# Attention's loads in another order on SyncE's queue: one weight block later, six weight blocks ahead of keys and values

## The chip, the cores and the metric

The kernel runs on one core of one Trainium2 chip. The metric is the device time of one execution in microseconds (us). Three executions of the kernel before took 513.55, 513.63 and 513.99 us; their median is 513.63 us.

## The reference, cut to what matters

Three stages follow one another: a decayed linear attention over 2 batches x 8 heads, a gated product through dense weights, and a mixture of 8 experts with top-1 routing.

```
# attention, in blocks of 64 positions
intra = (qb @ kb^T * Dmask) @ vb          inter = (qb * lam_pow) @ kv_state
out   = intra + inter                     kv_state = lam^64 * kv_state + (kb * rev_pow)^T @ vb
# dense stage, x is (1536, 512)
h = ((x @ w1) * (x @ w2)) @ w3            x2 = h @ w_out
# experts: argmax of x2 @ w_gate, capacity 384 rows each
out = gate_w * relu(xe @ e1) @ e2
```

## The kernel before, in words

**Attention** takes its 16 (batch, head) pairs two heads at a time, so eight iterations `it` = 0 to 7, each over all 768 positions. An iteration needs two loads of 768 KB, called by `load_qkv` (L304): `tqk` (queries and keys, transposed, L306) and `tkv` (keys and values, L308). Both have three buffers, so `tqk` and `tkv` of iteration `it + 2` are issued in iteration `it`, after the last use of the buffer by iteration `it - 1`. "Pair 4" below is the fourth pair of loads, that of iteration 3; it is issued in iteration 1.

An iteration has two halves. `part1(it)` multiplies queries by keys (L391), masks the scores (L400 on VectorE), and builds the states from the decayed keys `kd` (L413, L421). `part2(it - 1)` multiplies scores by values (L439), adds the state's part (L453), and splits the result into a rounded part `xth` (ScalarE, L462) and a rest `xtl` (VectorE, L463). The decayed keys `kd` of the next iteration are made on ScalarE from `tkv` (L362).

**Weights are prepared beside it.** The dense weights come as 64-bit numbers, in blocks of 512 KB (L122). The chunks stand in a list: blocks 0 to 7 are `woi` (w_out), blocks 8 to 23 `w3i`, then `w`. `Feed.load(n)` (L152) issues the next n blocks, on SyncE's queue like `tqk` and `tkv`. It keeps the list's order and stops where a block would need a staging buffer whose block has not been converted yet in program order: there are four such buffers, and blocks 0 to 3 have buffers of their own. `Feed.tick` (L166) moves every block in flight one step on and starts the next one. The steps of a block: two ScalarE instructions read it (L132, L133), one tick later two on VectorE (L135, L138) finish it and so free the buffer, one tick later ScalarE and GpSimd split it (L142, L143). For w_out blocks TensorE then transposes (L219), ScalarE copies (L222), and TensorE multiplies by the gate's weights (L227). `TICKS` (L37) places the ticks: none in iteration 0, one at the end of iteration 1, and from iteration 2 on one in the middle of `part1` and one at the end. So block 0 starts in iteration 1, blocks 1 and 2 in iteration 2, blocks 3 and 4 in iteration 3, and so on to blocks 11 and 12. `LOADS` (L36) says how many blocks are issued behind the pair loads of each iteration; block 0 is issued before the loop.

All engines work through their instructions in program order. SyncE's instructions are nothing but these loads, in the order in which the program calls them; an instruction that waits holds up all behind it. Every SyncE load also waits until the load eight places ahead of it, or nearly so, has landed.

**After attention** (from 59.56 us on) come the product w3 x w_out (L295 to L297), the gated stage, routing and the experts, all dense matmuls.

Of the kernel before, what the change touches and what calls it, by code (L numbers as in the profile page):

```python
# [32 lines left out]
NW = (2, 1, 1, 1, 1, 1, 1, 1)  # L33
HOOK = 6
OVER = 7
LOADS = (1, 2, 2, 2, 2, 2, 2, 0)  # L36
TICKS = ((0, 0, 0, 0), (0, 0, 0, 1)) + ((1, 0, 0, 1),) * 6 + ((0, 0, 1, 0),)  # L37
XBW = 265

# [2 lines left out]
def tile_moe_chain(ctx, tc, cap, qk, kv, w12, w3i, woi, wgi, e1i, e2i, c32, c16, zero, out):  # L42
# [21 lines left out]
    def bank():  # L64
        return ps.tile([P, 512], F32, tag="b", name="bank")
# [138 lines left out]
    feed = Feed()  # L204

    def run_bg(n=1):
        for _ in range(n):
            feed.tick()
# [29 lines left out]
    def u_ready(it):  # L238
        u = bank()
        for jb in range(4):  # L240
            nc.tensor.matmul(
                u[:, jb * NE : (jb + 1) * NE],
                it.up[:, jb * P : (jb + 1) * P],
                gsum,
                start=True,
                stop=True,
            )
        it.us = us = u[:, 0 : 4 * NE].rearrange("p (j e) -> p j e", e=NE)
        uh, ul = it.view(it.hi)[:, :, 512:520], it.view(it.lo)[:, :, 512:520]
        nc.vector.tensor_copy(uh, us)  # L250
        nc.vector.tensor_tensor(ul, us, uh.bitcast(F32), op=ALU.subtract)
# [13 lines left out]
    for w, e, j in turn[0:2] + turn[4:5] + turn[2:4] + turn[5:]:  # L265
        tag = min(until, key=until.get)
        it = Item((e1i, e2i)[w][e, j], "p3g" if tag == "x" else "ring", tag)
# [32 lines left out]
    with pool("att", 2, side="right") as ap, pool("att1", side="right") as a1:  # L300
        slots["att"] = ap
        loads = {}

        def load_qkv(it):  # L304
            tqk = ap.tile([P, 2, S], F32, tag="qk", name="tqk", bufs=3)
            nc.sync.dma_start(tqk, qk[it])  # L306
            tkv = ap.tile([P, 2, NC, P], F32, tag="kv", name="tkv", bufs=3)
            nc.sync.dma_start(tkv, kv[it])  # L308
            loads[it] = (tqk, tkv)
# [3 lines left out]
        dmask = a1.tile([P, 4, P], F32, name="dmask")  # L313
        nc.sync.dma_start(c32_sb, c32)
        load_qkv(0)
        load_qkv(1)
        feed.load(1)
        warm = tmp.tile([P, 512], F32, tag="t", name="warm").bitcast(F16)[:, 0:512]
# [38 lines left out]
        def decay_keys(it):  # L357
            if it == 8:
                return
            kds[it] = ap.tile([P, NC - 1, P], F32, tag="kd", name="kd", bufs=1)  # L360
            for h in range(2):
                nc.scalar.activation(  # L362
                    kds[it][:, :, h * 64 : h * 64 + 64],
                    loads[it][1][:, 0, 0 : NC - 1, h * 64 : h * 64 + 64],
                    AF.Copy,
                    scale=dmask[:, (it // 2 * 2 + h) % 4, P - 1 : P],
                )
# [63 lines left out]
        def part2(it, ticks, qs, at, st):  # L431
            pair, b = divmod(it, 2)
            tkv = loads[it][1]
            os = [bank(), bank()]
            for cc in range(NC):
                half, c = divmod(cc, 3)
                for h in range(2):
                    hs = slice(h * 64, h * 64 + 64)
                    nc.tensor.matmul(  # L439
                        os[half][hs, c * P : (c + 1) * P],  # L440
                        tkv[:, 1, cc, hs],
                        at[:, h, cc, :],
                        start=c == 0,
                        stop=cc == 0,
                        skip_group_check=True,
                    )
            for half, o in enumerate(os):
                for c in range(3):
                    cc = half * 3 + c
                    for h in range(2):  # L450
                        hs = slice(h * 64, h * 64 + 64)
                        if cc:
                            nc.tensor.matmul(  # L453
                                o[hs, c * P : (c + 1) * P],
                                st[hs, cc - 1, :],
                                qs[hs, cc, :],
                                start=False,
                                stop=True,
                                skip_group_check=True,
                            )  # L460
                xh, xl = xt[2 * b + half]
                nc.scalar.copy(xh[:, pair, :], o[:, 0:G])  # L462
                nc.vector.tensor_tensor(  # L463
                    xl[:, pair, :], o[:, 0:G], xh[:, pair, :].bitcast(F32), op=ALU.subtract
                )
                if half == 0:
                    run_bg(ticks[2])

        prev = None
        for it in range(8):  # L470
            cur = part1(it, TICKS[it])
            if prev is not None:
                part2(it - 1, TICKS[it], *prev)
            if it + 2 < 8:
                load_qkv(it + 2)
            prev = cur
            feed.load(LOADS[it])
            if it == 2:
                nc.scalar.dma_start(wg_sb, wgi)
            if TICKS[it][3]:  # L480
                feed.tick(mid=lambda: decay_keys(it + 1))
            elif it + 1 < 8:
                decay_keys(it + 1)
            if wo_it[0].done == 4 and not hasattr(wo_it[0], "us"):
                u_ready(wo_it[0])
# [401 lines left out]
    for e in range(NE):  # L887
# [12 lines left out]
        for s in range(nmain):  # L900
            acc = bank()
            ss = slice(s * P, (s + 1) * P)
            for fb in range(8):
                it = e2_it[2 * e + fb // 4]
# [90 lines left out]
```

## Time and profile before

| | us |
|---|---|
| median of three executions | 513.63 |
| the profiled execution | 513.23 |
| its span in the trace | 511.1 |
| TensorE busy in the span | 497.0 |
| ScalarE busy / VectorE busy | 242.7 / 265.0 |
| first matmul after attention (L295) | 59.56 |

The page gives busy time by engine, the span in forty slices, the queues, and the costliest groups of instructions. TensorE is busy for 97% of the span. Almost all the time it is not lies in the first 60 us, the attention, and in the last 10. What is asked here happens in the first 60 us, so the trace is read there by stretches and in order of time.

### The profile page before, as it was taken

How to read it: one execution, taken by the hardware profiler on the slowest of the kernel's cores; microseconds unless marked ns; L12 is line 12 of the kernel's file. 1: busy time of each engine (PE TensorE's matmuls, PEld its weight loads, DVE VectorE, ACT ScalarE, POOL GpSimd, SP SyncE). 2: the span in 40 equal slices, each digit the busy share in tenths (PEclk: the TensorE clock that was granted, in tenths of full speed). 3: DMA queues.
4: the chain of work that ended last, by engine and by line, in shares of the span. 5: the costliest groups of instructions: out<-in, count | busy, mean ns of one | idle time of the engine just before them, and what ended most of it. 6: DMA issues, size and time to landing. Idle time of an engine off the chain costs nothing. (4 is left out here: it accounts for less than half of the span.)

```text
span 511.1 us, 9558 instructions
## 1 busy us (share of the span) xinstructions
PE 497.0 (97%) x3805; PEld 468.5 (92%) x3805; DVE 265.0 (52%) x576; ACT 242.7 (47%) x485; POOL 126.5 (25%) x124
## 2 busy tenths in 40 slices
PE   7999999999999999999999999999999999999993
PEld 4888999999999999999999999989989898989892
DVE  4998885668333223322332463768474746647410
ACT  2697987789211221122112423656455555646310
POOL 4356564446200000000020004404313040410101
PEclk9999999999999999999999999999999999999998
DMA  8999466557911000100010215587665667564200
GB/s 323 415 410 379 150 223 215 182 193 239 332 39 43 1 0 23 43 1 0 13 53 0 83 65 163 191 272 251 217 214 206 232 203 259 167 241 165 81 1 34
DMA packets 24529, 80.80 MB, mean 158 GB/s; under 512 B 3642, under 2 KB 5692, under 8 KB 24480
## 3 DMA queue, kind: packets, MB, share of 16 engines
q1 hardware_dynamic: 18976, 70.35, 38.9%
q0 software_dynamic: 3344, 7.85, 4.7%
q10 hardware_dynamic: 2160, 1.94, 1.1%
q8 instruction: 32, 0.52, 0.5%
q14 instruction: 17, 0.14, 0.1%
HBM read 74.84 MB, written 10.54 MB: 167 GB/s over the span
## 5 line engine op out<-in xcount | busy, mean ns | idle before, releaser
L97 DVE TENSOR_TENSOR wlo<-st,whi 128x512 fp32r<-128x512 f32 x128 | 82.1, 685 | 16.8 <-ACT whi L95 16.7
L295 PE MATMUL bank<-xtl,whi 128*128 128x384 f32 x256 | 87.1, 340 | 0.0
L297 PE MATMUL bank<-xth,wlo 128*128 128x384 f32 x256 | 86.4, 337 | 0.0
L296 PE MATMUL bank<-xth,whi 128*128 128x384 f32 x256 | 85.8, 335 | 0.0
L95 ACT CAST whi<-st 128x512 fp32r<-128x512 f32 x128 | 73.0, 621 | 15.8 <-PE bank L297 10.9
L787 PE MATMUL bank<-xdl,whi 128*128 128x256 f32 x256 | 72.4, 283 | 1.1 <-PEq L834 0.8
L787 PE MATMUL bank<-xdh,whi 128*128 128x256 f32 x256 | 72.2, 282 | 0.0
L787 PE MATMUL bank<-xdh,wlo 128*128 128x256 f32 x256 | 72.1, 282 | 0.0
L143 POOL TENSOR_TENSOR wlo<-t,whi 128x512 fp32r<-128x512 f32 x40 | 51.9, 1297 | 52.1 <-ACT whi L142 46.5
L295 PE MATMUL bank<-wxl,gh 128*128 128x264 f32 (+1 forms) x192 | 55.9, 291 | 0.0
L296 PE MATMUL bank<-wxh,gh 128*128 128x264 f32 (+1 forms) x192 | 54.2, 282 | 0.0
L297 PE MATMUL bank<-wxh,gl 128*128 128x264 f32 (+1 forms) x192 | 54.1, 282 | 0.0
L564 DVE TENSOR_TENSOR a_sb<-bank,a_sb 128x384 f32<-128x384 f32 x32 | 17.8, 557 | 66.9 <-PE bank L297 66.3
L295 PE MATMUL bank<-wlo,hh 128*128 128x512 f32 x128 | 51.1, 399 | 0.0
L297 PE MATMUL bank<-whi,hl 128*128 128x512 f32 x128 | 50.3, 393 | 0.0
L787 PEld LDWEIGHTS bank<-xdl,whi 128*128 128x128 f32 x256 | 48.5, 189 | 1.9 <-PEq L834 1.2
L296 PE MATMUL bank<-whi,hh 128*128 128x512 f32 x128 | 50.0, 390 | 0.0
L800 DVE SCALAR_TENSOR_TENSOR hl<-bank,hh 128x512 fp32r<-128x512 f32 x32 | 22.1, 690 | 53.3 <-ACT hh L799 53.3
L718 POOL DMA_INDIRECT out_dram<-y,idx x16 | 16.1, 1006 | 134.3 <-ACT y L920 104.8
L787 PEld LDWEIGHTS bank<-xdh,whi 128*128 128x128 f32 x256 | 48.3, 189 | 0.3
L787 PEld LDWEIGHTS bank<-xdh,wlo 128*128 128x128 f32 x256 | 48.4, 189 | 0.0
L295 PEld LDWEIGHTS bank<-xtl,whi 128*128 128x128 f32 x256 | 48.1, 188 | 0.0
(109 smaller groups left out, 1003.2 us busy)
## 6 DMA issues: line engine op xcount, KB each, us to landing
st<-e1i SPq DMA_DIRECT2D x32, 512.0 KB, 5.2
st<-e2i SPq DMA_DIRECT2D x32, 512.0 KB, 4.0
st<-w3i SPq DMA_DIRECT2D x16, 512.0 KB, 4.7
st<-w SPq DMA_DIRECT2D x16, 512.0 KB, 4.1
tqk<-qk SPq DMA_DIRECT2D x8, 768.0 KB, 11.1
tkv<-kv SPq DMA_DIRECT2D x8, 768.0 KB, 9.3
st<-woi SPq DMA_DIRECT2D x8, 512.0 KB, 10.1
out_dram<-zero SPq DMA_DIRECT2D x1, 3072.0 KB, 14.3
```

What stands on the lines that cost most here:

```text
L95: nc.scalar.copy(h, s)
L97: nc.vector.tensor_tensor(lo, s, h.bitcast(F32), op=ALU.subtract)
L143: nc.gpsimd.tensor_tensor(lo, t, h.bitcast(F32), op=ALU.subtract)
L295: nc.tensor.matmul(acc, wh, rl, start=first, stop=False)
L296: nc.tensor.matmul(acc, wh, rh, start=False, stop=False)
L297: nc.tensor.matmul(acc, wl, rh, start=False, stop=last)
L564: nc.vector.tensor_tensor(a_sb, acc, a_sb, op=ALU.mult)
L718: nc.gpsimd.indirect_dma_start(out=out, out_offset=bass.IndirectOffsetOnAxis(ap=idx[:, col : col + 1], axis=0), in_=src, in_offset=None, b ...
L787: nc.tensor.matmul(o, w[:, k, :], x[:, k, :], start=m == 0 and k == 2 and x is xl, stop=m == 1 and k == 1 and w is lo, skip_group_check=True,)
L800: nc.vector.scalar_tensor_tensor(hl, acc, 0.0, hh.bitcast(F32), op0=ALU.max, op1=ALU.subtract)
```

## The change

`LOADS` gives iteration 1 one block instead of two and iteration 7 one instead of none. `load_qkv` gets an argument: that many blocks are issued between `tqk` and `tkv`. In iterations 3, 4 and 5 all blocks of the iteration (two) go there, so ahead of `tkv`; elsewhere they stay behind the pair.

```
-LOADS = (1, 2, 2, 2, 2, 2, 2, 0)
+LOADS = (1, 1, 2, 2, 2, 2, 2, 1)
...
-        def load_qkv(it):
+        def load_qkv(it, first=0):
             tqk = ap.tile([P, 2, S], F32, tag="qk", name="tqk", bufs=3)
             nc.sync.dma_start(tqk, qk[it])
+            feed.load(first)
             tkv = ap.tile([P, 2, NC, P], F32, tag="kv", name="tkv", bufs=3)
             nc.sync.dma_start(tkv, kv[it])
...
+            ahead = LOADS[it] if 2 < it < 6 else 0
             if it + 2 < 8:
-                load_qkv(it + 2)
+                load_qkv(it + 2, ahead)
             prev = cur
-            feed.load(LOADS[it])
+            feed.load(LOADS[it] - ahead)
```

SyncE's queue from pair 4 to pair 5 before (`st0_261` holds blocks 2 and 3, `st_347` block 4, `st_349` block 5; `tqk_257` and `tkv_259` are pair 4, the other two pair 5):

```order
L306 DMA tqk_257<-qk 128x1536
L308 DMA tkv_259<-kv 128x1536
L122 DMA st0_261<-woi 128x1024 x2
L306 DMA tqk_343<-qk 128x1536
L308 DMA tkv_345<-kv 128x1536
L122 DMA st_347<-woi 128x1024
L122 DMA st_349<-woi 128x1024
```

The same stretch of SyncE's queue after (`tqk_342` and `tkv_344` are now pair 5):

```order
L306 DMA tqk_257<-qk 128x1536
L309 DMA tkv_259<-kv 128x1536
L122 DMA st0_261<-woi 128x1024
L306 DMA tqk_342<-qk 128x1536
L309 DMA tkv_344<-kv 128x1536
L122 DMA st0_261<-woi 128x1024
L122 DMA st_347<-woi 128x1024
```

Block 3 has moved from ahead of pair 5 to behind it, and block 5 to the next iteration.

SyncE's queue around the last two pairs before (`tqk_545` and `tkv_547` are pair 7, `tqk_655` and `tkv_657` pair 8; `st_549` is block 8, `st_659` block 9, `st_661` block 10):

```order
L306 DMA tqk_545<-qk 128x1536
L308 DMA tkv_547<-kv 128x1536
L122 DMA st_549<-w3i 128x1024
L306 DMA tqk_655<-qk 128x1536
L308 DMA tkv_657<-kv 128x1536
L122 DMA st_659<-w3i 128x1024
L122 DMA st_661<-w3i 128x1024
```

The same after (`st_545` is block 7, `st_547` block 8, `st_657` block 9, `st_659` block 10; the pairs are `tqk_543`, `tkv_549` and `tqk_655`, `tkv_661`):

```order
L306 DMA tqk_543<-qk 128x1536
L122 DMA st_545<-woi 128x1024
L122 DMA st_547<-w3i 128x1024
L309 DMA tkv_549<-kv 128x1536
L306 DMA tqk_655<-qk 128x1536
L122 DMA st_657<-w3i 128x1024
L122 DMA st_659<-w3i 128x1024
L309 DMA tkv_661<-kv 128x1536
```

Blocks 9 and 10 now stand ahead of pair 8's `tkv`, blocks 7 and 8 ahead of pair 7's. The instructions of the other engines keep their order.

## Rows read from the trace of the kernel before

**Rows 1.** Part 2 of the page: DMA busy tenths in 40 slices of the span.

```profile
DMA  8999466557911000100010215587665667564200
```

**Rows 2.** Windows: length; PE, PEld, DVE, ACT, POOL busy (instructions); PEclk; DMA share; GB/s.

```profile
28.61:35.46 6.85, 6.84 (x105) 5.71 (x105) 6.02 (x12) 6.32 (x13) 4.68 (x4) 1.00 1.02 409
35.46:43.09 7.63, 7.63 (x113) 6.69 (x112) 7.42 (x15) 7.41 (x15) 4.37 (x3) 1.00 1.03 412
...
60.00:160.00 100.00, 100.00 (x741) 99.81 (x740) 58.05 (x122) 62.66 (x126) 39.04 (x31) 1.00 0.57 192
```

**Rows 3.** Waits of TensorE, 60 to 512 us: us in total, times, longest.

```profile
PE bank L787 <- PEq L834: 0.8, 1, 0.8
```

**Rows 4.** Waits of ScalarE, 16 to 60 us.

```profile
ACT bank L132 <- DMA st<-w3i: 2.6, 1, 2.6
```

**Rows 5.** Timeline of SyncE's queue: start us, us, engine, line, operation, out<-in, count.

```profile
15.03 0.33 SPq L308 DMA_DIRECT2D tkv<-kv  x1
15.40 0.90 SPq L122 DMA_DIRECT2D st<-woi  x2
...
20.11 0.33 SPq L308 DMA_DIRECT2D tkv<-kv  x1
20.48 1.04 SPq L122 DMA_DIRECT2D st<-woi  x2
...
34.34 0.33 SPq L122 DMA_DIRECT2D st<-w3i  x1
...
40.04 0.33 SPq L308 DMA_DIRECT2D tkv<-kv  x1
40.47 37.37 SPq L122 DMA_DIRECT2D st<-w3i  x15
```

**Rows 6.** DMA issues near 15.03, 15.40, 20.11, 40.47 us: KB each, us to landing.

```profile
tkv<-kv SPq DMA_DIRECT2D x1, 768.0 KB, 8.0
...
st<-woi SPq DMA_DIRECT2D x1, 512.0 KB, 8.9
...
tkv<-kv SPq DMA_DIRECT2D x1, 768.0 KB, 9.5
...
st<-w3i SPq DMA_DIRECT2D x1, 512.0 KB, 8.5
```

**Rows 7.** Timeline, 25.6 to 28.7 us: columns of rows 5, [idle before <-releaser].

```profile
25.62 0.61 ACT L142 CAST whi<-t 128x512 fp32r<-128x512 f32 x1
26.13 0.64 ACT L132 ACTIVATE bank<-st 128x512 f32<-128x512 f32 x1
...
27.59 1.09 PE L219 MATMUL bank<-c_sb,t 128*128 128x128 f32 x8
27.86 1.00 DVE L463 TENSOR_TENSOR xtl<-bank,xth 128x384 fp32r<-128x384 f32 x2
...
28.61 1.61 PE L391 MATMUL bank<-tqk 64*128 64x128 f32 x24
```

**Rows 8.** Timeline, 33 to 54 us, the same columns.

```profile
33.10 1.41 PE L453 MATMUL bank<-qs,state 64*64 64x128 f32 x20
...
37.61 1.03 PE L413 MATMUL bank<-tkv,kd 128*64 128x64 f32 x19
...
47.45 1.41 PE L453 MATMUL bank<-qs,state 64*64 64x128 f32 x20
...
48.96 0.65 ACT L132 ACTIVATE bank<-st 128x512 f32<-128x512 f32 x1 [2.63 <-DMA st<-w3i]
...
51.21 1.60 PE L391 MATMUL bank<-tqk 64*128 64x128 f32 x22 [0.92 <-DVE xtl L463]
...
53.31 0.82 PE L413 MATMUL bank<-tkv,kd 128*64 128x64 f32 x19
```

**Rows 9.** Windows at the end of the span, columns of rows 2.

```profile
503.00:504.00 1.00, 0.03 (x1) 0.00 (x0) 0.38 (x1) 0.47 (x1) 0.00 (x0) 1.00 0.00 0
...
506.00:507.00 1.00, 0.00 (x0) 0.00 (x0) 0.00 (x0) 0.00 (x0) 0.00 (x0) 0.55 0.38 146
```

## The prediction, made before the changed kernel ran

> **What bounds the kernel now.** I read the forty slices first. The DMA engines are busy nine tenths and more through slices two to four, the first 50 us, and far less behind [rows 1]. Next the windows: through attention the DMA share is 1.02 at 409 GB/s, so the queue never runs dry there, and ScalarE is busy for 6.32 of 6.85 us and 7.41 of 7.63 us of two iterations [rows 2]. Then TensorE behind attention: from 60 us on it is busy 100.00 of 100.00 us [rows 2], and its longest wait down to the end is 0.8 us [rows 3]. So whatever the change does to the end of attention moves the end of the kernel by the same amount; behind it nothing can hide or give back a shift.
>
> Inside attention two limits stand close together: ScalarE's chain, and the order in which the full queue delivers. The waits of ScalarE show where the second one wins: it waits 2.6 us once for a w3 block [rows 4], the one whose reading starts at 48.96 us [rows 8]. That is block 9: blocks 8 and 9 start at the end of iteration 5 and in iteration 6.
>
> The queue delivers in the order of issue. The `tkv` of pair 4 is issued at 15.03 us and lands 8.0 us later, at 23.0; block 2 is issued at 15.40 and lands 8.9 us later, at 24.3 [rows 5, 6]. The distance of 1.3 us is the block's own transfer: 524,288 B at 409 GB/s is 1.28 us. A `tqk` or `tkv` of 786,432 B takes 1.92 us. While the queue is full, a landing time is therefore set by the bytes ahead of it, whatever order those bytes have among themselves.
>
> **The change part by part.** Nothing is added or removed on the computing engines. Only landing times move.
>
> *Block 3 goes behind pair 5.* Before, the queue holds block 2, block 3, `tqk` and `tkv` of pair 5; after, block 2, `tqk`, `tkv`, block 3. These are the same bytes, so block 3 now lands when that `tkv` landed: issued at 20.11, 9.5 us to landing, 29.6 us [rows 5, 6]. The issue is no limit: block 3 is issued right behind the `tkv`, near 20.5 us, with some nine microseconds of transfers ahead. Its reader is ScalarE's L132 in iteration 3, which started at 26.13 without a wait, just as the instruction ahead of it ended (25.62 plus 0.61 is 26.23) [rows 7]. So ScalarE now waits from 26.2 to 29.6, 3.4 us. Behind it in ScalarE's order stand L133 and the two `xth` casts; VectorE's `xtl`, at 27.86, needs the casts, and TensorE's next scores, at 28.61, need the banks that `xtl` frees [rows 7]. All three engines stand still; TensorE has only the transposes of 27.59 to do, which end at 28.68. The whole chain moves by 3.4 us. What can it win back before the next wait? At most the idle time of ScalarE, its busiest engine, in the next two iterations: 14.48 us less 13.73 busy [rows 2], 0.75 us. It is idle there because it waits for the others, which move as well, so I take nothing back. Ends: 2.65 us, and 3.5 us with the re-start of VectorE behind the casts. Value: 3.4 us.
>
> *Blocks 5 to 10 ahead of three `tkv` loads.* Block 9 landed at 40.47 plus 8.5, 48.97 us [rows 5, 6]. It now stands ahead of the last `tkv`, so 1.92 us fewer bytes precede it: 47.05 us. Its reader was ready 2.63 us before 48.96, at 46.33 [rows 8], and with the 3.4 us above comes at 49.7. The wait of 2.63 us is gone, wholly. What was it worth? Not 2.63: while ScalarE stood, TensorE went on with L453 at 47.45, on which the casts depend in any case. Compare the same piece of two iterations: from L453 to L413 it took 37.61 less 33.10, 4.51 us, without a wait, and 53.31 less 47.45, 5.86 us, with it [rows 8]. The difference, 1.35 us, is my value. Ends: the 0.92 us that TensorE itself shows before L391 [rows 8], and the whole 2.63.
>
> *The `tkv` loads that come later.* Those of pairs 6 and 7 have one block more ahead of them than before, 1.28 us; their readers come 3.4 us later. That of pair 8 has two more, 2.56 us: it landed just ahead of block 9, at 47.7, and now lands at 50.2, while TensorE used its product at 53.31 [rows 8] and will do so about two microseconds later. No cost. Without the shift of 3.4 us, each would be near its reader.
>
> *Waits on SyncE.* Block 8 needs the buffer of block 4 and now stands ahead of pair 7's `tkv` and pair 8's `tqk`; blocks 9 and 10 stand ahead of pair 8's `tkv`. Block 8 was issued at 34.34, when its buffer came free [rows 5], so now at 37.7. The queue then still holds what ends with block 7: behind block 3 (29.6) come block 4, `tqk`, two blocks, `tkv`, `tqk`, block 7, or 4 x 1.28 + 3 x 1.92 = 10.9 us, so it lands until 40.5. With 2.8 us of work left the queue doesn't run dry, and those behind the wait are not late. No cost; if the cover went, the readers named above would still have some two microseconds.
>
> *Iteration 7's block* is issued a little earlier or later in a queue that is no longer full. Nothing.
>
> **Sum.** 3.4 less 1.35 is 2.05 us more. The profiled execution took 513.23 us, its span 511.1, with 2.1 us around it; it would take 515.3. The median is 0.40 us above that execution, so the median becomes 513.63 + 2.05 = 515.7 us.
>
> **The rivals.** *All of the old wait comes back.* If the engines are so tightly tied that ScalarE's idle 2.63 us was lost entirely, and ScalarE's 0.75 us is won back, the cost is 2.65 less 2.63, nothing; with 3.4, it is 0.8. The middle is 0.4 us, so 514.0. For it: ScalarE is nearly full. Against it: the comparison of the two iterations, and the 0.92 us.
>
> *Block 3 isn't late.* Were the queue to serve it ahead of the 1.5 MB of pair 5, or were the queue not full at 20 us, the wait at 26.2 would not arise; what is left is the old wait's 1.35 us: 512.3, faster. It decides at one point: whether block 3 lands by 26.2. Against it stand the DMA share of 1.02 and the landings in order, 1.3 us apart [rows 2, 6]. If only part of the lateness went, the balance lies at a wait of 1.35 us, block 3 landing at 27.6.
>
> *TensorE's clock falls in the new gap.* TensorE ends its transposes at 28.7 and has nothing until about 32. At the end of the span the last matmul is over in the window from 503, the granted clock is still 1.00 there, and in the window from 506 it is 0.55 on the mean [rows 9], so within it the clock goes to 1.2 GHz. A gap of about 3.3 us is as long as that stretch. An iteration's piece of 3 us of matmuls at half the clock would take 3 us more, half of which ScalarE's work hides: 1.5 us, so 517.2. Against it: before, the clock is 1.00 in all of attention [rows 2] and the gap is not longer. The Trainium skill, "TensorE: Matmul & The Clock Gate", under "HAM oscillation", says that a matmul kernel which stops for its loads between groups of matmuls is throttled in the stop and starts each group cold; by that rule the time would be this rival's and not the forecast's, and no run so far shows such a stop here.
>
> **How the numbers follow.** The forecast, 515.7, gets 0.72, by itself 514.8 to 516.3 (ends 2.65 less 1.9, and 3.5 less 0.92). The old wait coming back, 514.0: 0.12. The clock, 517.2: 0.08. Block 3 not late, 512.3: 0.06; 0.02 for anything unnamed, split. A measurement of this kernel can tell about 0.2%, 1.03 us: slower begins at 514.66, faster ends at 512.60. Slower is 0.72 and 0.08 with a little of the unnamed, 0.81; same is 0.12; faster 0.07. The range from 514.0 to 516.9 leaves out the clock, block 3 and a part of the second case.
>
> **What would show it right or wrong.** In the changed kernel's trace: a wait of ScalarE's L132 for a `woi` block of about 3.4 us, ending near 29.6; TensorE idle from 28.7 to about 32; no wait of L132 for a w3 block; the first L295 near 61.6 instead of 59.56; TensorE full behind it. It is wrong if block 3 lands early, if the wait for block 9 is replaced by one for a `tkv`, or if L295 starts before 60.6.

## The result, and the profile after

The changed kernel took 516.18 us (median of 6, 515.60 to 517.79) against 513.42 us (median of 6, 512.69 to 513.99): a ratio of 1.0060, with a 95% interval of 1.0050 to 1.0071. It is slower by 2.8 us, where 2.05 were forecast. The execution profiled below took 516.62 us with a span of 514.5.

The waits of ScalarE from 16 to 64 us (us in total, times, longest) answer to [rows 4]:

```profile
ACT bank L132 <- DMA st<-woi: 3.7, 2, 3.5
ACT xth L463 <- PE bank L454: 3.4, 7, 1.5
```

The wait for a w3 block is gone and one of 3.5 us for a w_out block is there. The casts wait for TensorE as long as before in sum; the line of before was:

```profile
ACT xth L462 <- PE bank L453: 3.5, 4, 2.9
```

New in it is the longest wait, 1.5 us, ahead of the cast at 38.12 (before, the longest stood ahead of the first cast, at 15.66). Now the timeline of SyncE's queue and of the engines from 20 to 38 us (start, us, engine, line, operation, out<-in, count, idle before); it answers to [rows 5] and [rows 7], with line numbers one or two higher:

```profile
20.29 0.33 SPq L309 DMA_DIRECT2D tkv<-kv  x1
20.67 0.90 SPq L122 DMA_DIRECT2D st<-woi  x2
...
25.37 0.60 ACT L142 CAST whi<-t 128x512 fp32r<-128x512 f32 x1
...
27.48 1.09 PE L219 MATMUL bank<-c_sb,t 128*128 128x128 f32 x8
28.50 0.48 PE L392 MATMUL bank<-tqk 64*128 64x128 f32 x2
...
28.91 0.42 SPq L122 DMA_DIRECT2D st<-woi  x1
...
29.48 0.62 ACT L132 ACTIVATE bank<-st 128x512 f32<-128x512 f32 x1 [3.51 <-DMA st<-woi]
...
31.07 1.02 DVE L464 TENSOR_TENSOR xtl<-bank,xth 128x384 fp32r<-128x384 f32 x2 [3.15 <-ACT xth L463]
...
31.30 1.08 ACT L222 COPY wt<-bank 128x512 f32<-128x512 f32 x2
...
31.68 1.84 PE L392 MATMUL bank<-tqk 64*128 64x128 f32 x22 [2.69 <-DVE xtl L464]
...
32.78 1.04 ACT L363 ACTIVATE kd<-tkv,dmask 128x320 f32<-128x320 f32 x2
...
34.46 1.34 PE L414 MATMUL bank<-tkv,kd 128*64 128x64 f32 x20
...
37.35 1.40 PE L454 MATMUL bank<-qs,state 64*64 64x128 f32 x20
```

This is the chain as forecast: ScalarE stands until 29.48, VectorE until 31.07, TensorE until 31.68. But the chain does not keep the whole shift. The same two instructions of ScalarE before:

```profile
28.50 1.07 ACT L222 COPY wt<-bank 128x512 f32<-128x512 f32 x2 [0.31 <-PE bank L219]
...
29.98 1.02 ACT L362 ACTIVATE kd<-tkv,dmask 128x320 f32<-128x320 f32 x2
```

ScalarE reads block 3 3.35 us later than before (29.48 against 26.13 [rows 7]), but makes `kd` only 2.80 us later (32.78 against 29.98). And then something more happens. From L392 to L454 TensorE takes 37.35 less 31.68, 5.67 us, where before it took 33.10 less 28.61, 4.49 us, with two matmuls more [rows 7, 8]. Windows over these microseconds (length; PE, PEld, DVE, ACT, POOL busy; PEclk; DMA share; GB/s) say why:

```profile
31.00:32.00 1.00, 0.32 (x4) 0.33 (x6) 0.94 (x2) 1.00 (x4) 0.00 (x0) 1.00 1.01 408
32.00:33.00 1.00, 1.00 (x21) 1.00 (x18) 0.87 (x3) 1.00 (x3) 0.02 (x1) 0.95 1.05 422
33.00:36.00 3.00, 3.00 (x36) 1.97 (x36) 2.98 (x6) 3.00 (x7) 3.00 (x3) 0.50 1.04 421
36.00:37.00 1.00, 1.00 (x20) 1.00 (x18) 0.51 (x1) 0.60 (x2) 1.00 (x2) 0.85 0.96 379
37.00:38.00 1.00, 1.00 (x18) 0.83 (x16) 0.91 (x2) 0.00 (x0) 0.64 (x1) 1.00 0.88 352
```

The granted clock is at 1.2 GHz (0.50) from about 32.9 to 36.3 us: one tenth of the window from 32 and three tenths of that from 36. In [rows 2] it was 1.00 throughout. Behind attention nothing has changed but the start, 62.73 us instead of 59.56. TensorE's timeline there, with the L454 that started at 47.45 before [rows 8], and the window behind it:

```profile
51.70 1.41 PE L454 MATMUL bank<-qs,state 64*64 64x128 f32 x20
...
62.73 0.39 PE L295 MATMUL bank<-wlo,whi 128*128 128x256 f32 x1
```

```profile
64.00:164.00 100.00, 100.00 (x741) 99.81 (x740) 58.10 (x125) 62.52 (x127) 38.55 (x31) 1.00 0.57 191
```

The start of L454 moved by 4.25 us, that of L295 by 3.17 and the span by 3.4.

### The profile page after: what moved, and what is told of

It is laid out like the page before. It is cut to its first block, busy times and chain, and to the rows that moved or that the text cites. A ratio compares the mean times of both kernels' runs of the same rounds, so it can differ in the third digit from the quotient of the medians.

```text
span 514.5 us, 9559 instructions
## 1 busy us (share of the span) xinstructions
PE 499.0 (97%) x3805; PEld 469.5 (91%) x3805; DVE 265.3 (52%) x576; ACT 242.9 (47%) x485; POOL 127.4 (25%) x124
## 5 line engine op out<-in xcount | busy, mean ns | idle before, releaser
L295 PE MATMUL bank<-xtl,whi 128*128 128x384 f32 x256 | 87.1, 340 | 0.0
L295 PE MATMUL bank<-wxl,gh 128*128 128x264 f32 (+1 forms) x192 | 55.9, 291 | 0.0
L295 PE MATMUL bank<-wlo,hh 128*128 128x512 f32 x128 | 51.1, 400 | 0.0
L297 PEld LDWEIGHTS bank<-xth,wlo 128*128 128x128 f32 x256 | 48.1, 188 | 0.0
```

What stands on the lines that cost most here:

```text
L295: nc.tensor.matmul(acc, wh, rl, start=first, stop=False)
L297: nc.tensor.matmul(acc, wl, rh, start=False, stop=last)
```

## The experiments

Theory A: block 3's lateness makes the wait, the wait makes the loss, and TensorE's clock falls in the gap that the wait leaves. Theory B: the blocks ahead of `tkv` cost the time. The first four kernels ran beside 23 executions of the kernel before, median 513.46 us.

**Only the first part** (from the changed kernel; block 3 behind pair 5, nothing ahead of a `tkv`):

```
-            ahead = LOADS[it] if 2 < it < 6 else 0
+            ahead = 0
```

> Only the first part: one block fewer behind pair 4 (LOADS as in the changed kernel), no block ahead of a tkv. Theory A (the late block 3 is the whole loss, with TensorE's clock falling in the gap that it makes): as the changed kernel, 515.7 to 516.6 us, against 513.4 before; ScalarE waits 3.4 to 3.6 us for a woi block until about 29.5, and does not wait for a w3 block, since block 9 lands at 49.0 and its reader comes at 49.7 or later. Theory B (blocks ahead of tkv cost the time, by late tkv loads or by waits on SyncE): close to before, 513.0 to 514.0.

Measured: 517.50 us, ratio 1.0073 (1.0056 to 1.0090). So the loss does not need the blocks ahead of `tkv`; theory B is out. The median is 1.3 us above the changed kernel's, which I had not expected (the intervals of the two ratios overlap), and there is a wait for a w3 block. Its timeline of SyncE and windows of the same columns as above:

```profile
28.35 0.33 SPq L306 DMA_DIRECT2D tqk<-qk  x1
37.88 0.33 SPq L309 DMA_DIRECT2D tkv<-kv  x1
38.26 0.42 SPq L122 DMA_DIRECT2D st<-woi  x1
```

```profile
36.00:37.00 1.00, 1.00 (x32) 1.00 (x28) 0.49 (x2) 0.77 (x2) 1.00 (x2) 1.00 0.69 270
37.00:38.00 1.00, 1.00 (x20) 0.83 (x18) 1.00 (x2) 0.49 (x1) 1.00 (x1) 1.00 0.20 76
38.00:39.00 1.00, 1.00 (x20) 0.95 (x18) 0.28 (x1) 0.48 (x1) 0.01 (x1) 1.00 0.48 104
```

Pair 7's `tkv` waits on SyncE for its buffer, which the late chain frees at 37.9 instead of 33.2, and block 7 waits behind it although nothing holds it. The queue runs dry: a DMA share of 0.20 at 37 us, where it is 0.88 in the changed kernel, which issued block 7 at 28.91. All later loads come later, and ScalarE waits 0.68 us for block 9. Yet up to the end of attention the trace shows next to no loss by this: block 3 was read 0.34 us later than in the changed kernel (29.82), L454 came 0.38 later (37.73), and L295 0.40 later. The rest stands far behind attention:

```profile
63.13 0.39 PE L295 MATMUL bank<-wlo,whi 128*128 128x256 f32 x1
...
326.20 0.68 PE L759 MATMUL bank<-c_sb,xga 128*128 128x128 f32 x4 [1.02 <-DMA xga<-xa_d,idx]
```

The profiled span is 1.5 us longer than the changed kernel's, and 1.02 us of it is this wait of TensorE for a gather of the experts. The profiles of the kernel before and of the changed kernel have no such wait, that of the next kernel has one of 0.84 us. So what the second part earns by letting blocks pass a `tkv` that must wait is not shown.

**Only the second part** (blocks ahead of `tkv`, `LOADS` as before):

```
-LOADS = (1, 1, 2, 2, 2, 2, 2, 1)
+LOADS = (1, 2, 2, 2, 2, 2, 2, 0)
```

> Only the second part: LOADS as before, the blocks of iterations 3, 4 and 5 ahead of their tkv. Theory A: block 3 is not late (no wait of ScalarE at 26 us); the tkv of pair 6 has two blocks more ahead of it and lands 2.56 us later, at 38.9, while its reader on ScalarE comes at 36.8, so a wait of 2.0 us there; the old wait for block 9 (worth 1.35 us) goes; 514.1 us, at most 0.8 us over before. Theory B: the loss is here, 515.5 to 516.5. If the order ahead of tkv brings what it takes from block 9's wait and nothing is late: 512.1.

Measured: 514.24 us, ratio 1.0021 (1.0009 to 1.0034): 0.8 us over before, where 514.1 us was expected (the twelve executions spread from 513.83 to 515.93). Its waits of ScalarE show the one that was named, at pair 6's `tkv`, and no w3 block:

```profile
ACT kd L363 <- DMA tkv<-kv: 2.5, 2, 1.9
```

So this part alone trades the wait for block 9, 2.6 us, for a shorter one that costs more:

```profile
49.48 1.41 PE L454 MATMUL bank<-qs,state 64*64 64x128 f32 x20
...
60.51 0.39 PE L295 MATMUL bank<-wlo,whi 128*128 128x256 f32 x1
```

L454 comes 2.03 us later than the 47.45 of before, and 1.08 of it comes back by L295, 0.95 later than before. Both parts together do not cost the sum of the two (4.0 and 0.8 us in the medians; 3.57 and 0.95 in the start of L295, against 3.17): in the changed kernel no wait for a `tkv` is longer than 0.4 us, so the late chain of the first hides the late `tkv` of the second.

**Block 3 between `tqk` and `tkv` of pair 5**, 1.92 us earlier than in the changed kernel:

```
-            ahead = LOADS[it] if 2 < it < 6 else 0
+            ahead = (0, 0, 1, 2, 2, 2, 0, 0)[it]
```

> The changed kernel with block 3 between tqk and tkv of pair 5, so 1.92 us earlier: it lands at 27.6. Theory A: the wait of ScalarE falls from 3.5 to 1.5 us, TensorE's gap to about 1.2 us, and its clock stays at 2.4 GHz; the wait costs what the old one for block 9 was worth, so 513.6 us (513.0 to 514.2), the balance point of the prediction. Theory B: unchanged order ahead of the other tkv loads, so still 515.5 to 516.5. If the size of the wait does not matter but that it is there: over 515.

Measured: 513.67 us, ratio 1.0008 (0.9997 to 1.0018). Block 3's landing sets the time, and the balance lies where it was forecast (L295 at 59.60, against 59.56 before). Its ScalarE and TensorE:

```profile
27.70 0.64 ACT L132 ACTIVATE bank<-st 128x512 f32<-128x512 f32 x1 [1.58 <-DMA st<-woi]
```

```profile
29.94 1.60 PE L392 MATMUL bank<-tqk 64*128 64x128 f32 x22 [0.93 <-DVE xtl L464]
```

The 22 matmuls take 1.60 us here and 1.84 in the changed kernel: behind a wait of 0.93 us the clock did not fall.

**Matmuls into TensorE's gap.** The first attempt put in too many:

```
         for it in range(8):
+            if it == 4:
+                wgap = psi.tile([P, 512], F32, tag="i", name="wgap")
+                for _ in range(20):
+                    nc.tensor.matmul(wgap[:, 0:P], ident, ident, start=True, stop=True)
             cur = part1(it, TICKS[it])
```

> The changed kernel with 20 matmuls of the identity (128x128, into a bank that nothing else uses yet) put on TensorE into the gap of iteration 4, where it waits for xtl. They fill some 2.6 of about 3 us. If the fallen clock costs time: granted clock 0.995 instead of 0.993 in the mean, no stretch at 0.50 between 32 and 37 us, and about 1.1 us less than the changed kernel, 515.1 (514.7 to 515.6) in every run, with little spread. If the clock costs nothing, since ScalarE's chain hides it: 516.1 as the changed kernel. If the filling delays the scores: over 516.5.

Measured: 516.19 us, no gain. The clock stayed at 1.00, but the filling took 4.63 us and ran over the gap, so that the scores began at 32.96 instead of 31.68: what the clock gave was spent. This settled nothing, so it was done again with 11 in place of 20, beside the changed kernel itself. The chip was another one: there the kernel before took 515.57 us (26 executions), so ratios to it are what counts. Up to the end of attention, though, the traces can be laid side by side: the last kernel below, which computes like the one before, starts its L391 there at 28.62, 35.46 and 43.09 us, the kernel before at 28.61, 35.46 and 43.09 here. The difference stands behind attention: from L295 to the end of the span the earlier traces took 451.5 to 453.1 us, those of the second chip 453.1 to 454.2.

> The changed kernel itself, beside the next one on the same chip: 516.1 us (515.6 to 517), mean clock 0.993, as measured first.

Measured: 519.66 us, ratio 1.0074 (1.0056 to 1.0092), 4.1 us over before. The clock was low for longer in the profiled execution, by its windows from about 30.8 to 37.7 us, and L295 started at 64.02:

```profile
30.50:31.00 0.50, 0.00 (x0) 0.00 (x0) 0.00 (x0) 0.50 (x2) 0.00 (x0) 0.84 1.01 410
...
32.00:36.00 4.00, 4.00 (x36) 2.96 (x38) 3.87 (x8) 4.00 (x9) 2.89 (x3) 0.50 1.02 413
...
37.50:38.00 0.50, 0.50 (x12) 0.50 (x10) 0.50 (x1) 0.00 (x0) 0.27 (x1) 0.84 0.79 315
```

```profile
64.02 0.39 PE L295 MATMUL bank<-wlo,whi 128*128 128x256 f32 x1
```

> The changed kernel with 11 matmuls of the identity in TensorE's gap of iteration 4 (20 of them took 4.63 us and ran 1.3 us over the gap's end, so 11 take 2.55 us and end near 31.0, ahead of 31.7). If the fallen clock costs time by itself: no stretch at 0.50 between 32 and 37 us, L295 at 61.5 instead of 62.7, 1.2 us less than the changed kernel in the same call, 514.9 (514.4 to 515.4). If ScalarE's chain hides the slow matmuls: no difference, 516.1.

Measured: 517.03 us, ratio 1.0033 (1.0020 to 1.0047), 1.5 us over before and 2.6 less than the changed kernel beside it. The wait of ScalarE is unchanged; the lines of its timeline (the trace has two records for each of the 11 matmuls) and two windows:

```profile
28.29 2.62 PE L475 MATMUL wgap<-c_sb 128*128 128x128 f32 x22
...
29.45 0.64 ACT L132 ACTIVATE bank<-st 128x512 f32<-128x512 f32 x1 [3.54 <-DMA st<-woi]
...
31.68 1.60 PE L392 MATMUL bank<-tqk 64*128 64x128 f32 x22 [0.35 <-DVE xtl L464]
...
35.91 1.40 PE L454 MATMUL bank<-qs,state 64*64 64x128 f32 x20
...
61.41 0.39 PE L295 MATMUL bank<-wlo,whi 128*128 128x256 f32 x1
```

```profile
30.00:32.00 2.00, 1.65 (x15) 1.34 (x15) 0.94 (x2) 2.00 (x6) 0.00 (x0) 1.00 1.03 410
32.00:34.00 2.00, 2.00 (x35) 1.47 (x33) 1.87 (x5) 2.00 (x5) 1.02 (x1) 1.00 1.04 415
```

L392 starts at 31.68 as in the changed kernel, but L454 follows after 4.23 us instead of 5.67. L295 comes at 61.41, 1.32 us ahead of the changed kernel's first profile, 2.61 ahead of its second, on the same chip, and 1.85 behind before. That splits the loss: 1.85 us by the two waits at full clock, and 1.3 us in one profile and 2.6 in the other by the clock.

**Toward a better kernel.** If the old wait for block 9 is worth 1.35 us, bringing only that block forward must gain it. First the kernel before with blocks 9 and 10 ahead of the last `tkv`:

```
-            ahead = LOADS[it] if 2 < it < 6 else 0
+            ahead = 2 if it == 5 else 0
```

> The kernel before (its LOADS) with blocks 9 and 10 ahead of the last pair's tkv only. Theory A: block 3 is in time, the tkv of pairs 6 and 7 land as before, block 9 lands at 47.05, its reader, ready at 46.3, waits 0.7 us, which TensorE's L453 hides: 1.35 us less than before, 512.1 (511.7 to 512.6), faster than both. If the old wait was worth its whole 2.63 us less 0.7: 511.5. If TensorE's end of attention is set by something else: 513.4.

Measured: 514.40 us, ratio 0.9977 (0.9967 to 0.9986), 1.2 us less than before; L295 at 58.37 instead of 59.56, of which 0.11 us was there before block 9 is read (L414 at 45.29, against 45.40). ScalarE still waits for block 9 as computed:

```profile
46.91 0.65 ACT L132 ACTIVATE bank<-st 128x512 f32<-128x512 f32 x1 [0.70 <-DMA st<-w3i]
48.11 0.48 ACT L463 CAST xth<-bank 128x384 fp32r<-128x384 f32 x1
```

```profile
58.37 0.39 PE L295 MATMUL bank<-wlo,whi 128*128 128x256 f32 x1
```

Then block 9 ahead of the last `tqk` too (from the kernel before):

```
+            ahead = 1 if it == 5 else 0
+            feed.load(ahead)
             if it + 2 < 8:
                 load_qkv(it + 2)
             prev = cur
-            feed.load(LOADS[it])
+            feed.load(LOADS[it] - ahead)
```

> The kernel before with block 9 alone moved ahead of the last pair's tqk and tkv, the rest as before. Block 9 lands near 45.1, no wait of ScalarE for it at all; the last tqk is held back by block 9's buffer until 37.3 instead of 34.8, but lands with the queue's order at 47.0, its scores being due at 49.8. Theory A: as the kernel with blocks 9 and 10 ahead of tkv, 512.1, since ScalarE waits for TensorE there in any case. If the remaining 0.7 us counted too: 511.4. If the wait on SyncE costs: 513.4 or more.

Measured: 514.30 us, ratio 0.9972 (0.9960 to 0.9984), 1.4 us less than before. The wait for block 9 is gone and one for TensorE of the same size has taken its place:

```profile
46.25 0.67 ACT L132 ACTIVATE bank<-st 128x512 f32<-128x512 f32 x1
46.86 0.68 ACT L133 ACTIVATE st<-st 128x512 int32<-128x512 uint16 x1
48.24 0.48 ACT L462 CAST xth<-bank 128x384 fp32r<-128x384 f32 x1 [0.70 <-PE bank L453]
```

```profile
58.51 0.39 PE L295 MATMUL bank<-wlo,whi 128*128 128x256 f32 x1
```

The cast starts at 48.24 with no wait for the load and at 48.11 with 0.70 us of it, so those 0.70 us are worth nothing. Both kernels beat the one before and the changed one; between the two the intervals show no difference.

## Why the prediction was right, and where it was short

- *The wait for block 3.* Forecast 3.4 us until 29.6; measured 3.51 until 29.48. The rule that only the bytes ahead count held: the `tkv` and block 3 changed places and block 3 landed when the `tkv` had.
- *The chain wins nothing back.* This was wrong by 0.6 us. I let the whole chain move by 3.4 us and set the 0.75 us that could come back at nothing, because the others "move as well". `kd` moved by 2.80 us, before the clock fell, and with the gap filled L454 moved by 2.81 (35.91 against 33.10). One piece shows how: before, ScalarE waited 0.31 us at L222 for TensorE's transposes; in the changed kernel TensorE made them while ScalarE stood, and that wait is gone. Where the rest came back was not followed.
- *The old wait was worth 1.35 us.* It was worth 1.1. In the piece where I read it, it did come back: the changed kernel's L454 at 51.70 is 4.25 us late, the L414 after it (56.16, against 53.31) 2.85. But by L295 0.3 us of that was lost again, 3.17. So the wait for block 9 was worth 1.08 us there, and as much in the second part alone (2.03 less 0.95) and with the gap filled (2.93 at L454 less 1.85). The two last kernels give it by itself: 1.08 (1.19 less the 0.11 of before block 9) and 1.05 us in the start of L295, 1.2 and 1.4 us in time. That is between two of the three readings, TensorE's own wait (0.92) and the same piece in two iterations (1.35), and far from ScalarE's (2.63).
- *No cost from the later `tkv` loads.* Right in the changed kernel, and for the reason given: without the shift, pair 6's `tkv`, with two blocks more ahead of it, costs a wait of 1.9 us.
- *The queue doesn't run dry.* Right in the cost. Block 7, issued at 28.91, landed 11.4 us later, at 40.3, where the forecast had 40.5, and block 8 went out at 37.26 instead of 37.7. But the share fell to 0.88 at 37 us. It stays that high because block 7 stands ahead of the waiting `tkv`; where it doesn't it is 0.20. I had counted the second part's work as block 9 alone; what the fuller queue is worth in time no run shows.
- *TensorE's clock.* This step failed. I left it out of the sum and gave the fall a chance of 0.08, because the gap would be "not longer" than the stretch at the end of the span. It is in fact shorter, 2.69 us without a matmul, and the clock fell in both profiles of the changed kernel and in that of the first part alone, whose gap is 3.06 us; it stayed at 1.00 through attention in all profiles without such a gap, those with the gap filled among them. The missing term is 1.3 us in the first profile, which with 1.85 makes the 3.17 of L295, and 2.6 us in the second. In the six executions measured first the mean clock goes with the time: 515.60 us at 0.995, 516.04 to 516.62 at 0.993, 517.79 at 0.990; in the first part alone it does not (516.29 us at 0.992, 518.12 at 0.994). The Trainium skill says in "TensorE: Matmul & The Clock Gate", under "HAM oscillation", that work behind a stop for a load starts cold, and so spoke against my weight. The second profile agrees with it, 0.50 from about 30.8 us and matmuls again from 31.81; in the first the matmuls of 31.68 began at full clock, and the fall came at about 32.9.
- *Two slips on paper.* "2.65 less 1.9" is 0.75, which gives 514.4 and not the 514.8 at the low end of the forecast, and the 1.9 is worked out nowhere. And the DMA engines are as busy again in the eleventh slice of [rows 1], about 128 to 141 us, well behind attention. Neither moves the 515.7.

So the forecast came within half a microsecond of 516.18, but in part by luck. The chain moved 0.6 us less and the old wait gave back 0.3 less, so that the net cost of the waits, 1.85 us, was close to the 2.05 of the sum; and the clock added what I had left to a rival, whose price of 1.5 us was near the 1.3 measured. The measured time lies between the two cases, since the rival's 1.5 us on top would have been 517.2. On the second chip the same change cost 4.1 us, which on top of 513.63 would be 517.7, above the 516.9 that the range ended with.

One reading about the part behind attention was too firm. Nothing there hides a shift, but it does not always take the same time: TensorE's wait for the gather is absent in two profiles, 0.84 and 1.02 us in two others, so a difference of a microsecond between single executions need not come from attention.

## What to carry to other kernels

In a full transfer queue, write down the landing time of each load from the bytes ahead of it and hold it against its reader's start; moving one load earlier is paid by all it passes, and there the slack of each must be looked up. A wait is worth what the next engine in the chain loses by it, not its length: here 2.63 us were worth 1.1, the last 0.70 of them nothing, and the new one of 3.5 us was worth 2.8. Bring forward only the load that is late, and where a change opens a gap of TensorE like the 2.7 us here, count with matmuls at half clock behind it.

## What the runs showed of the hardware that I had not expected

- A stop of TensorE of 2.69 us was followed by 3.4 us or more at 1.2 GHz, though the granted clock had been 1.00, 2.4 GHz, through the 28 us ahead of it; a stop of 0.93 us was not. Eleven matmuls in the stop kept the clock at 1.00.
- The fall came in one profile at about 32.9 us, over a microsecond after matmuls had resumed, and in another at about 30.8, ahead of them, where it lasted twice as long, 6.8 us; its cost was 1.3 us in the first (L295 at 62.73 against 61.41 with the gap filled) and 2.6 us in the second (64.02 against 61.41), as much as between the medians on that chip.
- The same kernel before took 513.46 us on one chip and 515.57 on another, most of the 2.8 us under study; only kernels run beside each other can be compared.
